# Filler products in free PSUM tiles, and turns at the port of VectorE and GpSimd, in a scheduled two-layer attention kernel

## The chip, the cores and the metric

The kernel runs on one core of a Trainium2 chip. The metric is the device time of one execution in microseconds (us). A core has five engines with an instruction list each: TensorE (PE in the profile, with its weight loads as PEld), VectorE (DVE), ScalarE (ACT), GpSimd (POOL) and SyncE (SP), which here only issues DMAs. Every list is worked off in the order in which the kernel wrote it, and engines wait for each other on semaphores.

## The reference

Four blocks follow each other on x of 2048 tokens by 512 columns (bf16): A, B, A, B, each with a layer norm ahead and a residual sum behind it. "Layer" L below is one pair of A and B. There are 32 heads of 16 columns.

```python
# A: attention inside 4 segments of 512 tokens, with a memory of the segments before
for s in range(4):
    p = softmax(qs @ ks.T / 4 + causal_mask)
    a_dot = p @ vs
    a_mem = (phi(qs) @ M) / (phi(qs) @ z + 1e-6)      # phi(t) = t + 1 if t > 0 else exp(t)
    o = g * a_mem + (1 - g) * a_dot                    # g = sigmoid(beta), by head
    M += phi(ks).T @ vs;  z += phi(ks).sum(tokens)
x = x + concat(o) @ wo
# B: linear attention over all tokens, features from softmax of +p and of -p
phi_q, phi_k = feat(q @ w_phi), feat(k @ w_phi)
kv, z = phi_k.T @ v, phi_k.sum(tokens)
x = x + ((phi_q @ kv) / (phi_q @ z + 1e-6)) @ wo
```

In B, kv and z run over all tokens, so no query of B can be finished before the last key has been added.

## The kernel before

Tokens come in 16 tiles of 128, four to a segment. For each layer the kernel projects q, k and v of a segment (`a_proj`, labels K, Q, V), works through its four tiles (`a_att`), adds the output projection to x (`out_proj`), normalizes again (`ln`) and adds B's keys of the segment to KV32 (`b_keys`). After the fourth segment the queries of B follow, four chunks of four tiles (`b_query`), mixed with the norms and projections of the next layer's A. This is called the pass to queries below; there is one for each layer.

In `a_att` a score product of TensorE (pQ,pK) fills a PSUM tile of 128x1024, ACT takes its exponential into SBUF (L603), GpSimd masks the diagonal tiles (L1035), TensorE multiplies with the values (pV), and VectorE divides (L649, L1063). In segment 0 of layer 0 the scores need a q masked by head (Q4), which VectorE makes at L969. VectorE's copies of the layer A weights into their working order are L804, the gate on the value weights L792. In `b_query` the denominators (Rz) come first. From them ACT and VectorE make weights (L1213 to L1219); the numerators (Rkv) are computed per tile, copied by ACT, multiplied at L1236, transposed by TensorE against ident or by a DMA, and projected with WB_o. All matmuls of these steps are recorded at L593. PSUM holds four tiles of 128x1024 (pool pD, in the profile D), with caps by class: at most two live tiles of class S, to which scores and numerators belong.

The order is not written by hand. Each step is recorded as an operation with a price in ns for each engine that may take it, with what it reads and writes. `Graph.forward` then plays all engines forward in time: at each moment every free engine takes the ready operation of highest priority whose tiles can be had. Priorities come from a backward pass, and are then shifted by a list of random seeds (STEPS). What comes out is an order for each engine, and the choice of engine for copies that ACT or VectorE may do (`evac`). `emit` writes the lists with a semaphore wait for each dependence. Prices and planned times are not in the program.

Two rules of `forward` matter here. One is on the port shared by VectorE and GpSimd: a VectorE operation marked `port` isn't started while GpSimd is at work, and GpSimd not while such an operation runs. When both are free, VectorE is asked first, as it stands first in ENGS. The other is on TensorE's activity: if fewer than 60% of the columns possible (KEEP) were streamed in the last 3 us (WINDOW), the next operation with columns of 64 or more repeats its first product until that is made up, at most 1024 columns a pair (MORE):

```python
lack = KEEP * WINDOW * 2.4 - streamed - o.cyc
o.again = min(MORE * 512 // o.unit, max(0, int(-(-lack // o.unit))))
```

At the start of the program `warm` (L917) sends 56 products of a constant tile of ones (onesb), 64x512 each, into a PSUM tile.

## Time and profile before

| | |
|---|---|
| median of 8 runs | 547.04 us (544.58 to 552.81) |
| the profiled execution | 547.03 us, of which the span of instructions is 545.3 us |
| mean granted TensorE clock | 0.984 |
| busy: PE, ACT, DVE, POOL | 473.9, 470.7, 440.0, 232.1 us |
| POOL waits for the exponentials of ACT (L1035) | 156.4 us |
| ACT waits for TensorE at L603 | 46.2 us in 56 waits |
| moved by DMA | 31.79 MB, 58 GB/s in the mean |

The page divides the span into 40 slices of 13.6 us; a digit is the busy share of an engine there in tenths, and in the row PEclk the share of the full TensorE clock that was granted. Time that an engine idles matters only where a later step waits for that engine.

### The profile page before, as it was taken

To read this page: it belongs to the slowest core of one execution; us is meant where nothing else is said; L and a number is where in the kernel's file an instruction comes from. 1 tells how busy PE (TensorE), PEld (TensorE's weight loads), DVE (VectorE), ACT (ScalarE), POOL (GpSimd) and SP (SyncE) were. 2 spreads that over 40 slices of the span, in tenths; PEclk is the share of its full clock that TensorE was granted. 3 is DMA by queue.
4 is the path that set the end of the run, shared out by engine and by line. 5 is a ranking of instruction groups with operands and counts; after the bars stand their busy time and mean duration, and the time that the engine had idled before them with its cause. 6 is when DMAs were issued, how large, how long until landed. Compare 5 with 4: busy or idle time off the path is not lost.

```text
span 545.3 us, 25035 instructions
## 1 busy us (share of the span) xinstructions
PE 473.9 (87%) x11338; PEld 286.2 (52%) x11338; DVE 440.0 (81%) x853; ACT 470.7 (86%) x547; POOL 232.1 (43%) x401
## 2 busy tenths in 40 slices
PE   8868788899898899997998888997989998899785
PEld 3325344555464565656753655454555555465674
DVE  6898998997986987776786989897788797878771
ACT  3959988999999999677787989999989999886884
POOL 5645767445653753100326634763463384310000
PEclk9979999999999999997899999999999999999999
DMA  7155343622211211000224445324021112100265
GB/s 213 31 183 133 71 83 73 81 49 61 42 33 32 33 32 31 4 1 5 32 63 83 64 96 74 70 42 80 31 42 25 40 23 41 26 9 3 52 119 127
DMA packets 90521, 31.79 MB, mean 58 GB/s; under 512 B 77584, under 2 KB 90416, under 8 KB 90416
## 3 DMA queue, kind: packets, MB, share of 16 engines
q1 hardware_dynamic: 90352, 30.17, 27.4%
q8 instruction: 89, 1.46, 1.2%
q14 instruction: 16, 0.13, 0.1%
q0 software_dynamic: 64, 0.02, 0.0%
HBM read 6.32 MB, written 2.10 MB: 15 GB/s over the span
## 4 chain that ended last, share of the span: by engine, by line
PE 43%; DVE 23%; ACT 21%; DMA 8%; issue 4%; SPq 1%; POOL 0%; DVEq 0%; ACTq 0%
PE D L593 41%; ACT p L603 19%; DMA p<-p 7%; DVE p L1063 2%; DVE p L612 2%; DVE p L869 2%; DVE stats L848 2%; PE D L917 2%; DVE pQ L969 1%; DVE X L1096 1%; DVE p L1236 1%; DVE pS L1141 1%; DVE pS L649 1%; DVE pK L612 1%; SPq L975 1%
## 5 line engine op out<-in xcount | busy, mean ns | idle before, releaser
L603 ACT ACTIVATE p<-D 128x1024 bf16<-128x1024 f32 (+1 forms) x420 | 400.5, 1025 | 50.0 <-PE D L593 46.2
L1035 POOL TENSOR_SCALAR_AFFINE_SELECT p<-p 128x512 bf16<-128x512 bf16 x256 | 163.8, 666 | 156.8 <-ACT p L603 156.4
L593 PE MATMUL D<-pQ,pK 64*128 64x512 bf16 x676 | 124.3, 379 | 15.8 <-ACT p L603 11.2
L593 PE MATMUL D<-pV,p 64*128 64x34 bf16 x5312 | 94.0, 177 | 5.0 <-issue 1.7
L593 PEld LDWEIGHTS D<-pV,p 64*128 64x128 bf16 x5312 | 82.8, 93 | 19.2 <-issue 5.6
L593 PEld LDWEIGHTS D<-pQ,pK 64*128 64x128 bf16 x676 | 32.7, 94 | 49.1 <-ACT p L603 27.1
L856 POOL TENSOR_SCALAR rstd<-mv 128x1 f32<-128x1 f32 x60 | 16.6, 280 | 93.5 <-DVE mv L849 92.0
L1063 DVE TENSOR_TENSOR p<-D,pS 128x256 bf16<-128x256 f32 x112 | 47.2, 422 | 2.9
L593 PE MATMUL D<-WA_o,p 64*128 64x256 bf16 x532 | 40.2, 270 | 8.4 <-DMA p<-p 5.3
L848 DVE BATCH_NORM_STATS2 stats<-X 128x6 f32<-128x512 bf16 x64 | 43.4, 685 | 4.3 <-DMA X<-in_A_x_dram 2.3
L1141 DVE TENSOR_REDUCE pS<-p 128x64 f32<-128x1024 bf16 (+1 forms) x36 | 38.7, 1087 | 6.7 <-ACT p L603 6.7
L593 PE MATMUL D<-WB_o,p 64*128 64x256 bf16 x522 | 40.4, 278 | 4.3 <-DMA p<-p 1.9
L1161 DVE TENSOR_TENSOR pT<-D,pT 128x1024 bf16<-128x1024 f32 x32 | 38.7, 1213 | 5.5 <-PE D L593 5.1
L593 PE MATMUL D<-WA_v,pX 64*128 64x512 bf16 x258 | 34.8, 392 | 6.1 <-DVE pV L612 4.1
L858 POOL TENSOR_TENSOR rstd<-rstd,mhalf 128x1 f32<-128x1 f32 x60 | 36.6, 612 | 3.4
L593 PE MATMUL D<-WB_k,pX 64*128 64x512 bf16 (+1 forms) x288 | 34.6, 353 | 3.2 <-issue 1.7
L593 PEld LDWEIGHTS D<-WA_o,p 64*128 64x128 bf16 x532 | 23.5, 94 | 22.0 <-DMA p<-p 8.5
L593 PE MATMUL D<-WB_v,pX 64*128 64x512 bf16 (+1 forms) x290 | 34.0, 354 | 0.8 <-DVE pT L649 0.4
L593 PE MATMUL D<-pX,WA_q 64*128 64x512 bf16 x228 | 29.7, 382 | 5.3 <-DVE p L1243 2.1
L1096 DVE TENSOR_TENSOR X<-X,D 128x512 bf16<-128x512 bf16 x32 | 21.8, 682 | 15.3 <-PE D L593 14.8
L649 DVE RECIPROCAL pS<-D 128x32 f32<-128x32 f32 (+1 forms) x64 | 20.7, 324 | 15.3 <-PE D L593 14.9
L593 PE MATMUL D<-pX,WB_q 64*128 64x512 bf16 x256 | 32.1, 376 | 0.1
(114 smaller groups left out, 681.7 us busy)
## 6 DMA issues: line engine op xcount, KB each, us to landing
pQ<-p SPq DMA_DIRECT2D x112, 32.0 KB, 1.8
out_dram<-X SPq DMA_DIRECT2D x16, 128.0 KB, 2.0
X<-in_A_x_dram SPq DMA_DIRECT2D x3, 512.0 KB, 4.9
pX<-in_B_wqkv_dram SPq DMA_DIRECT2D x3, 512.0 KB, 5.7
p<-p SPq DMA_TRANSPOSE x76, 2.7
pX<-p SPq DMA_TRANSPOSE x54, 2.4
X<-in_A_x_dram SPq DMA_DIRECT2D x4, 128.0 KB, 2.6
pX<-in_A_wk_dram SPq DMA_DIRECT2D x2, 256.0 KB, 3.6
```

Of the source, the lines that this page charges most:

```text
L593: ins = e.matmul(out_ap, lhsT, rhs, start=st, stop=sp, tile_position=(basep(lhsT), 0))
L603: return self.g.op({"act": (dur, lambda e: e.activation(out_ap(), in_ap(), func, scale=scale))}, reads, writes, opens, label=label)
L612: "dve": ((340 if fast else n / 0.96 + 65), lambda e: e.tensor_copy(out_ap(), in_ap()))}
L649: return e.reciprocal(o, i)
L848: v(lambda e: e.bn_stats(self.stats[:, t, :], self.X[:, t, :]), 602, [R("X", t)], [R("st", t)], label="bn")
L856: v(lambda e: e.tensor_scalar(rs, self.mv[:, t, 1:2], LN_EPS, None, op0=ALU.add), 170, [R("mv", t)], [R("rstd", t)], eng="pool", label="rstd")
L858: v(lambda e: e.tensor_tensor(rs, rs, self.mhalf[:], ALU.pow), 540, [R("rstd", t), R("mhalf")], [R("rstd", t)], eng="pool", label="rstd")
L1035: v(lambda e, pt4=pt4: e.affine_select(pt4(), pt4(), [[0, 4], [1, 128]], ALU.is_ge, 0.0, base=0, channel_multiplier=-1), 560, [PT], [PT[hh ...
L1063: v(lambda e, pvv=pvv, rden=rden, part=part, dst=dst, k=k: e.tensor_tensor(part(dst), pvv()[:, :, k, :, 0:16], rden()[:, :, k, :, None].to ...
L1096: self.v(lambda e: e.tensor_tensor(xt(), xt(), res(), ALU.add), 602, [R("X", t), ps], [R("X", t)], label="res")
L1141: fn = lambda e, sgn=sgn, ev=ev, Z=Z, nz=nz: e.tensor_reduce(Z.t[:, sgn * nz:(sgn + 1) * nz], ev().rearrange("p (h d) -> p h d", d=16), AX ...
L1161: v(lambda e, Vt=Vt, src=src, vt=vt: e.tensor_tensor(vt(Vt, 0, 16), src(), vt(Vt, 16, 17).to_broadcast([128, 2, 2, 2, 16, 8]), ALU.mult), ...
```

## The change

1. When TensorE finds nothing to do in the plan, after the first 12 us, and a PSUM tile is free, under 70% (IDLE) of the columns were streamed in the last 3 us, and no TensorE operation that could have its tiles becomes ready within 216 ns (FILL), the planner puts in a filler: two products of the tile of ones, 64x512 each, written into the free tile. The tile isn't reserved by this; the filler waits for the tile's last readers.
2. When VectorE and GpSimd are both free, the one is asked first that did not hold the port last (TURNS).
3. Some prices change: a load issued on SP from 470 ns to 520 (or 620 each, in groups), two kinds of copy on ACT and VectorE.
4. The list STEPS is another one, with 137 seeds in place of 108.

```diff
+TURNS = {"pool": ENGS, "dve": ("pe", "act", "pool", "dve", "sp")}
-WINDOW, KEEP, MORE = 3000.0, 0.6, 2
+WINDOW, KEEP, MORE, IDLE, FILL, START = 3000.0, 0.6, 2, 0.7, 216.0, 12000.0
+    def filler(self, now):
+        pool, make, deps = self.idle
+        o = Op()
+        o.id, o.deps, o.tiles, o.opens, o.hard, o.kind, o.label = 0, set(deps), [], [], (), "c", "fill"
+        t = Tile(pool, "fill")
+        t.base, t.slot = pool.base[pool.free[0]], pool.free[0]
+        o.tiles = [t]
+        o.ch = {"pe": (FILL, lambda e: make(e, t.t))}
...
-            for e in ENGS:
-                if free[e] > now + 1e-9 or not ready[e]:
+            for e in TURNS[port_last]:
+                if free[e] > now + 1e-9 or not (ready[e] or e == "pe"):
                     continue
...
+                    if e == "pe" and self.idle and now > START and len(self.idle[0].free) > 0:
+                        while seen_pe and seen_pe[0][0] < now + FILL - WINDOW:
+                            streamed -= seen_pe.pop(0)[1]
+                        if streamed < IDLE * WINDOW * 2.4 and not any(r < now + FILL and ops[i].eng is None and can_alloc(ops[i]) for r, i in soon[e]):
+                            o = self.filler(now)
+                            seen_pe.append((o.end, 512.0))
+                            streamed += 512.0
+                            free[e] = o.end
...
-                    held_port = o.end
+                    held_port, port_last = o.end, e
+                elif e == "pool" and o.kind == "c":
+                    port_last = e
...
-    def evac(self, out_ap, in_ap, n, reads, writes, opens=(), label="", fast=False):
-        ch = {"act": (n / 1.2 + 51, lambda e: e.activation(out_ap(), in_ap(), ACT.Copy)),
+    def evac(self, out_ap, in_ap, n, reads, writes, opens=(), label="", fast=False, slow=0):
+        ch = {"act": (slow or n / 1.2 + 51, lambda e: e.activation(out_ap(), in_ap(), ACT.Copy)),
...
-            dur = 780.0 if eng == "pool" else 470.0
+            dur = 780.0 if eng == "pool" else 520.0 if n == 1 else 620.0
...
+    def fill(self, e, ps):
+        for b in range(2):
+            ones = self.onesb[64 * b:64 * b + 64, :]
+            ins = e.matmul(ps[:, 512 * b:512 * b + 512], ones, ones[:, None, :].to_broadcast([64, 4, 128]), start=True, stop=True, tile_position=(64 * b, 0))
+        return ins
...
+        self.g.idle = self.pD, self.fill, list(self.R("onesb").w)
         self.g.schedule(self.pools, ROUNDS, OFF)
```

In the changed program the fillers are recorded at L953, and the line numbers behind `filler` stand some 28 to 35 lines further on (L593 becomes L621, L603 becomes L631, L969 becomes L1003).

## The prediction

> **What bounds the kernel now.** I read the page's busy times and slices first, then the waits, then windows around every dip in the clock row, then the timeline and the chain there.

> ```profile
> span 545.3 us, 25035 instructions
> PE 473.9 (87%) x11338; PEld 286.2 (52%) x11338; DVE 440.0 (81%) x853; ACT 470.7 (86%) x547; POOL 232.1 (43%) x401
> PEclk9979999999999999997899999999999999999999
> ACT p L603 <- PE D L593: 46.2, 56, 4.5
> PEld D L593 <- DMA pX<-p: 6.6, 2, 4.6
> ```

> No engine is saturated. ACT idles for 545.3 − 470.7 = 74.6 us, and most of that (46.2 us) is the exponential waiting for TensorE, once for 4.5 us. The kernel is held by hand-overs between engines, so the question is where they are worst. The clock row dips in its third digit (27 to 41 us, where the mean is 0.75) and in digits 19 and 20 (245 to 273 us). The mean clock of 0.984 means 0.016 x 545.3 = 8.7 us of clock lost, that is about 17 us at half speed. Windows cut at the edges:

> ```profile
> 31.30:35.40 4.10, 0.01 (x3) 0.03 (x1) 4.10 (x10) 1.94 (x2) 1.29 (x2) 0.81 0.27 46
> 35.40:40.80 5.40, 5.40 (x27) 2.15 (x29) 4.22 (x10) 1.94 (x2) 1.23 (x2) 0.51 1.06 370
> 245.40:252.50 7.10, 4.89 (x316) 4.58 (x316) 5.08 (x14) 6.28 (x12) 0.00 (x0) 0.99 0.02 5
> 252.50:262.70 10.20, 8.77 (x240) 7.27 (x240) 5.15 (x11) 5.36 (x10) 0.00 (x0) 0.51 0.07 16
> ```

> The columns are length, then busy time of PE, weight loads, DVE, ACT and POOL, then the granted clock. TensorE does nothing for 4.1 us and then works 5.4 us without a pause at half clock. Around 245 us, where layer 0 passes from its last keys to its queries, it is busy 4.89 of 7.10 us with tiny matmuls, and then spends 10.2 us at half clock, busy 86% of it. These are the two places that the fillers can reach. What stands in the first:

> ```profile
> 35.37 0.16 PEld L593 LDWEIGHTS D<-WA_v,pX 64*128 64x128 bf16 x4 [4.55 <-DMA pX<-p]
> 37.75 1.02 ACT L603 ACTIVATE p<-D 128x1024 bf16<-128x1024 f32 x1 [4.46 <-PE D L593]
> ```

> The value projection of segment 1 stands in TensorE's list ahead of scores of segment 0. It waits for DMA transposes, everything behind it waits too, and ACT loses 4.46 us.

> **The change part by part.**

> *Fillers.* In the built program of the changed kernel, 88 matmuls of 64x512 (44 fillers of two) are added: 26 among the scores of segment 0 in layer 0, 28 at the first pass to queries, 2 in layer 1, 28 at the second pass to queries and 4 near the end. They replace repeats: Rkv products fall from 680 to 512, ident products from 348 to 238, WB_o from 522 to 512; score products (pQ,pK) rise from 676 to 698. A filler is not in the trace. The nearest rows are WA_v products of the same shape: 16 of them took 1.89 us and 8 took 1.03, so one more costs 0.86/8 = 0.108 us; the upper end is the warm-up row (9.1 us for 56, 0.163 each, partly cold). With 0.108: fillers 88 x 0.108 = +9.5 us, score repeats 22 x 0.108 = +2.4. What is dropped:

> ```profile
> 246.64 2.01 PE L593 MATMUL D<-Rkv,p 64*128 64x64 bf16 x124 [0.25 <-DVE Rkv L1114]
> 507.37 0.87 PE L593 MATMUL D<-ident,p 64*128 64x64 bf16 x48 [0.37 <-DVE p L1236]
> ```

> That is 16 ns per Rkv and 18 ns per ident product: 168 x 0.016 = 2.7, 110 x 0.018 = 2.0, and 10 WB_o about 0.6 us. TensorE's net work is +6.6 us. It is nearly free only where it lies in idle time: PE has 71 us of that. A filler waits for the last reader of its PSUM tile (an ACT or DVE copy), as does the product behind it on the same tile; so it adds no wait, but it stands 0.2 to 1.1 us in front of that product. Queued behind are the numerators (Rkv), and for them waits ACT's copy, then the VectorE multiply at L1236. In a plan that runs late this is lost time; that cover gone, it costs the full 9.5 us.

> *First pass to queries.* What full clock is worth there, the trace itself shows, since the same stage runs a second time at clock 1.00:

> ```profile
> 245.44 0.96 PE L593 MATMUL D<-Rz,p 64*128 64x8 bf16 x64 [0.83 <-DVE Rz L1117]
> 261.39 1.06 PE L593 MATMUL D<-WB_o,p 64*128 64x256 bf16 x8
> 502.58 0.95 PE L593 MATMUL D<-Rz,p 64*128 64x8 bf16 x64
> 513.51 0.61 PE L593 MATMUL D<-WB_o,p 64*128 64x256 bf16 x8
> ```

> From the first Rz product to the end of the third half of an output projection: 262.45 − 245.44 = 17.0 us against 514.12 − 502.58 = 11.5 us. The first passage holds 104 more Rkv products (1.7 us), 48 more ident (0.9) and 64 fewer Rz (−1.0), so 5.5 − 1.6 = 3.9 us is the clock. As a bound from above: 8.77 us of PE at half clock would shrink like WB_o's 1.06 to 0.61, by 3.7 us, and 1.8 us more if the waits before it go too: 5.5. From below: 0, should it dip again. Taken −4.0. The repeats dropped there (some 100 pairs, 3.5 us) and the 14 fillers (3.0 us) cancel.

> [...] But at 252.5 us the longest gap before the fall is under 2 us: small products alone did not hold the clock. [...]

> *The start.* The diff reprices a load on SP (470 to 520 or 620 per issue), and the built order puts the segment 1 value projection behind 15 score tiles of segment 0 where it stood behind 7, and behind the 13 fillers. SP is moved too: weight loads of layer B now stand between the four transposes of segment 1, and the first transposes of weights follow earlier. The 4.46 us of ACT wait, with the 1.1 and 0.5 that follow under half clock, is 6.1 us at most. VectorE is next: the chain before 35.3 us is its masks and copies (L969, L804), and it is busy 12.28, 12.42 and 11.27 us of the three slices from 13.6 to 54.5 us, leaving 4.9 us. So the gain is between −4.9 and, if the masks come later than the scores, +2. VectorE's work there hardly changes: one gate of WA_v comes from GpSimd (+1.2), three weight copies leave for ACT (−1.4). Taken −3.0. Late next: the masks of Q4.

> *Second pass and end.* The clock was 1.00 there, so 32 fillers can gain nothing: +3.5 us of PE work against about 1.4 us of repeats gone, in a stretch where PE is busy 33.1 of 43.0 us. Bounds 0 and +2.1; taken +0.5. SP's last transposes change from four in a row to three, a store and one: within ±1, taken 0. The very last filler only follows the last projection: 0.

> *Turns at the port.* Nothing in the program enforces a turn: the planner reorders, and no semaphore is added. What overlap costs shows in one row at two times:

> ```profile
> 21.26 0.41 DVE L969 TENSOR_TENSOR pQ<-p 128x512 bf16<-128x512 bf16 x1
> 25.46 0.85 DVE L969 TENSOR_TENSOR pQ<-p 128x512 bf16<-128x512 bf16 x1
> ```

> The slower one runs beside GpSimd's mask. Over all rows (16 of L969 at 582 against 410 ns, 48 of L869 at 496 against 400, L905 and L1067) the surplus is about 10 us of VectorE, some 3 of it before 68 us where VectorE is on the path. Bounds −3 and +3, taken 0.

> *The rest of the order.* Nearly every list is permuted, since the planner's seeds change. Work per engine hardly moves (DVE +2.4, ACT −0.6 us from the copies that change sides), and both engines have 75 us or more idle. Over 41 to 218 and 300 to 491 us ACT's idle slices sum to about 22 us; a permutation may win or lose a quarter of that, ±5. Taken −0.5, as two of the copies now priced dearer leave ACT (0.74 us each, L611): an estimate from these rows, no more.

> Sum: −4.0 − 3.0 + 0.5 + 0 − 0.5 = −7.0 us on a span of 545.3: 538.3, with 1.7 around it 540.0. The profiled execution took 547.03, the median 547.04, so no shift is needed.

> **The rivals.**
> *Slower: fillers in front of due work.* All 44 sit on PSUM tiles that a numerator or score is about to use. If ACT's copies come earlier than planned or the inputs are ready, each filler is a pure delay: +9.5 us, less 4.7 us of repeats dropped, no clock won: 547 + 5 = 552. It decides only where the clock isn't won, and then from 4.7 us of filler on the path, as much as the dropped repeats give back. For it: that product carries no wait of its own in several groups. Against: ACT and DVE idle at the passes because they wait on each other (the 1.8 us before 252.98 is not PE's).
> *The clock falls all the same, or the next wait takes the gain.* Fillers come in bursts of 0.2 to 1.1 us, and 14 of them add 7,168 columns a row half over 15 us. If that is too thin, the first pass gives 0, and a start held by VectorE gives −1: 546. For it: the repeats were meant for the same and failed. Then the change doesn't do what it says.
> *The order wins more.* Both places give their bounds (−4.9, −5.5) and the permutation −5: about 531.

> **How the numbers follow.** Forecast 0.60 (own range 533 to 546, mostly faster); next wait or clock 0.17 (mostly same); fillers or a worse order on the path 0.19 (547 to 553); order wins more 0.04. Within 0.5% is 544.3 to 549.8, about what a measurement of this kernel can tell from no change. Faster: 0.55 + 0.05 + 0.04 = 0.64. Same: 0.05 + 0.11 + 0.01 = 0.17. Slower: 0.18 + 0.01 = 0.19. The range runs from the best case, 531, to the price of the slower one, 552.

> **What would show it.** Right: clock at or above 0.99 with no slice under 0.9 between 27 and 41 and between 245 and 273 us; the 4.5 us ACT wait gone; first Rz to third half projection in 12 to 13.5 us; L969 still above 500 ns. Wrong: the clock restored with the end unmoved (the wait moved on), TensorE's wait on ACT at L953 followed at once by Rkv rows with ACT idle (fillers in the way), or a gain that lies between 45 and 220 us (the order).

## The result, and the profile after

The changed kernel takes 543.47 us in the median (540.65 to 550.45) where the kernel before took 548.19 beside it: a ratio of 0.9928 (0.9906 to 0.995), some 3.9 us less. Measured again on another chip it is 0.9913 (0.9874 to 0.9952). Chips differ by up to 3.7 us in the median of the kernel before (547.10 to 550.78 us beside the experiments), so kernels are compared by their ratio to the kernel before of the same chip. Ratios leave disturbed runs out, so where a kernel's runs spread widely its ratio lies below what its median says (e9 and e16 below). The profiled execution after was one of the longer of its kernel: 548.0 us. Its page (the same rows as shown of before) and its waits (us in all, times, longest):

```profile
span 546.2 us, 24666 instructions
PE 479.0 (88%) x11156; PEld 284.4 (52%) x11156; DVE 430.0 (79%) x854; ACT 468.4 (86%) x547; POOL 234.8 (43%) x400
PEclk9978999999999999999999999899999999999899
...
ACT p L631 <- PE D L621: 49.4, 53, 4.2
PE D L621 <- issue: 10.2, 9, 3.7
```

The dip of the clock row at 245 to 273 us is gone, the one at 27 to 41 us is not, and there are new ones in digits 4, 26 and 38: half clock at 43.9 to 47.4, 351.1 to 354.6 and 515.0 to 518.4 us, where before ran at full clock. VectorE has lost 10 us of work, and the span hardly shows it. ACT waits as long as before. The pass to queries has changed in kind (window of after from the first Rz product to the end of the third half projection; then the timeline inside):

```profile
249.41:259.52 10.11, 9.41 (x352) 7.27 (x352) 6.94 (x17) 9.93 (x18) 0.00 (x0) 1.00 0.02 5
...
250.53 1.24 PE L953 MATMUL D<-onesb 64*128 64x512 bf16 x10
253.31 0.26 PE L621 MATMUL D<-Rz,p 64*128 64x8 bf16 x8 [0.21 <-issue]
254.54 1.25 PE L953 MATMUL D<-onesb 64*128 64x512 bf16 x10
258.92 0.60 PE L621 MATMUL D<-WB_o,p 64*128 64x256 bf16 x8
```

TensorE is busy 9.41 of 10.11 us at full clock: 17.0 us have become 10.1. So 6.9 us were won here, and this execution's span shows none of it. A table by stage, from the starts and ends in the traces (us; "again" is a second profile of the changed kernel, the last column an experiment told of below):

| stage | before | after | again | old order, shifted |
|---|---|---|---|---|
| start to the end of the second sum into X | 58.8 | 58.9 | 54.3 | 59.1 |
| to the first Rz product, layer 0 | 186.6 | 190.5 | 189.7 | 186.8 |
| to the third half projection | 17.0 | 10.1 | 10.0 | 11.5 |
| to the first Rz product, layer 1 | 240.1 | 243.8 | 244.2 | 236.4 |
| to the end | 42.7 | 42.9 | 44.3 | 39.3 |

The changed order gives back 3 to 4 us in each of the two long stages, and its start differs by 4.6 us between two executions of one program.

### The profile page after: what moved, and what is told of

Its sections match the earlier page's. It is cut to its first block, busy times and chain, and to the rows that moved or that the text cites. A ratio compares the mean times of both kernels' runs of the same rounds, so it can differ in the third digit from the quotient of the medians.

```text
span 546.2 us, 24666 instructions
## 1 busy us (share of the span) xinstructions
PE 479.0 (88%) x11156; PEld 284.4 (52%) x11156; DVE 430.0 (79%) x854; ACT 468.4 (86%) x547; POOL 234.8 (43%) x400
## 4 chain that ended last, share of the span: by engine, by line
PE 49%; ACT 23%; DVE 11%; DMA 10%; issue 3%; POOL 2%; SPq 1%; ACTq 0%
PE D L621 47%; ACT p L631 20%; DMA p<-p 7%; DMA pX<-p 3%; PE D L945 2%; DVE p L1097 2%; POOL p L1069 1%; DVE p L640 1%; SPq L1009 1%; DVE X L1130 1%; DVE pS L677 1%; DVE stats L876 1%; DVE pS L1175 1%; DVE pT L1195 1%; DVE p L897 1%
## 5 line engine op out<-in xcount | busy, mean ns | idle before, releaser
L631 ACT ACTIVATE p<-D 128x1024 bf16<-128x1024 f32 (+1 forms) x420 | 399.5, 1028 | 53.4 <-PE D L621 49.4
L621 PE MATMUL D<-pQ,pK 64*128 64x512 bf16 x698 | 129.1, 385 | 11.9 <-ACT p L631 10.1
L621 PE MATMUL D<-pV,p 64*128 64x34 bf16 (+1 forms) x5312 | 94.4, 177 | 9.1 <-issue 3.8
L621 PEld LDWEIGHTS D<-pV,p 64*128 64x128 bf16 x5312 | 82.8, 93 | 23.1 <-issue 10.0
L884 POOL TENSOR_SCALAR rstd<-mv 128x1 f32<-128x1 f32 x60 | 18.1, 304 | 101.9 <-DVE mv L877 101.9
L621 PEld LDWEIGHTS D<-pQ,pK 64*128 64x128 bf16 x698 | 34.1, 94 | 43.9 <-ACT p L631 24.0
L621 PE MATMUL D<-WA_o,p 64*128 64x256 bf16 x534 | 40.2, 271 | 10.9 <-DMA p<-p 8.0
L621 PE MATMUL D<-WB_o,p 64*128 64x256 bf16 x512 | 39.2, 274 | 6.6 <-DMA p<-p 4.9
L621 PE MATMUL D<-WA_v,pX 64*128 64x512 bf16 x256 | 33.9, 385 | 6.1 <-issue 3.7
L621 PE MATMUL D<-WB_k,pX 64*128 64x512 bf16 (+1 forms) x288 | 34.2, 353 | 4.5 <-DMA pX<-p 3.1
L621 PEld LDWEIGHTS D<-WA_o,p 64*128 64x128 bf16 x534 | 22.6, 94 | 27.1 <-DMA p<-p 12.4
L621 PE MATMUL D<-WB_v,pX 64*128 64x512 bf16 (+1 forms) x288 | 33.5, 353 | 0.9 <-ACT p L631 0.4
L621 PE MATMUL D<-pX,WB_q 64*128 64x512 bf16 x256 | 32.5, 376 | 0.1
L621 PE MATMUL D<-pX,WA_q 64*128 64x512 bf16 x224 | 29.3, 377 | 3.1 <-issue 1.6
```

The source lines that it names most:

```text
L621: ins = e.matmul(out_ap, lhsT, rhs, start=st, stop=sp, tile_position=(basep(lhsT), 0))
L631: return self.g.op({"act": (dur, lambda e: e.activation(out_ap(), in_ap(), func, scale=scale))}, reads, writes, opens, label=label)
L884: v(lambda e: e.tensor_scalar(rs, self.mv[:, t, 1:2], LN_EPS, None, op0=ALU.add), 170, [R("mv", t)], [R("rstd", t)], eng="pool", label="rstd")
```

## What the timeline of before had shown all along

The two rows of before that matter most were not read rightly in the prediction. Here they are, with their neighbours (timeline, PE alone; "issue" means that the engine waited for nothing that the profile shows):

```profile
249.25 0.29 PE L593 MATMUL D<-Rkv,p 64*128 64x64 bf16 x8 [0.60 <-issue]
...
250.83 0.35 PE L593 MATMUL D<-ident,p 64*128 64x64 bf16 x12
252.99 1.14 PE L593 MATMUL D<-ident,p 64*128 64x64 bf16 x36 [1.81 <-issue]
...
255.44 0.65 PE L593 MATMUL D<-Rz,p 64*128 64x8 bf16 x36
256.99 0.54 PE L593 MATMUL D<-Rz,p 64*128 64x8 bf16 x28 [0.91 <-issue]
```

Three times TensorE stops in the middle of a group (12 and 36 products of one transpose, 36 and 28 of one denominator). Nothing in the program waits there. Number TensorE's weight loads, products and semaphore waits in the order of their start: the three stand at numbers that leave 193 over a multiple of 256. So do, within two, 107 of the 129 stops of 0.5 us or more inside a group in all 20 traces of this case (score groups left out); 15 of the other 22 are one stop of the changed kernel and its variants at 22 us. The DMA part of the page of before, and of its window from 250 to 252 us, point to the cause:

```profile
q8 instruction: 89, 1.46, 1.2%
```
```profile
DMA packets 1, 0.02 MB, mean 8 GB/s; under 512 B 0, under 2 KB 0, under 8 KB 0
...
q8 instruction: 1, 0.02, 3.9%
```

1.46 MB in 89 packets are 16.4 KB each, and TensorE's 22,866 instructions in this trace (11,338 loads, as many products, 190 that wait or drain) by 256 are 89.3: by these counts TensorE's own list arrives by DMA, in blocks of 256 instructions. The only packet of that window is one of them. In the DMA records it starts at 250.37 us, 1.1 us after the block before it was entered (249.25), lands at 251.60, and TensorE goes on at 252.98. At the nine pauses of before (they are counted below) the packet starts 0.6 to 1.7 us after the block ahead was entered, and TensorE goes on 1.2 to 1.6 us after it has landed, so that the new block begins 3.1 to 4.2 us after the previous one. The trace doesn't say what a packet holds; that it is the next block is read from these times. The same block can pause in one execution and not in another: at one place after waited 1.40 us for a packet that started 2.8 us late (186.43 us), and in its second profile, where the packet started at once, not at all.

Below, a "block pause" is a gap of at least 0.5 us between the starts of two TensorE instructions at such a number, where the 256 before took under 4 us. Before has 9 of them, 10.3 us in all; after 5, 6.7 us; the second profile of after 3, 4.4 us. They come where short products use up the list fast: at the nine of before the 256 instructions ahead took 1.7 to 3.3 us without the pause, and 124 Rkv products passed in 2.01 us are, with their loads, 248 instructions. Fillers of 512 columns use it up more slowly: 10 of their products, with the loads 20 instructions, took 1.24 us in after. But every product added or dropped also moves all later block starts to other places; the last two experiments separate that from everything else.

## Experiments

There are four theories. *Clock*: the fillers hold the clock. *Order*: the gain is the new order's. *In the way*: fillers stand in front of due work. *Blocks* (later): what counts is where the block starts fall. The expectations number them: theory 1 is always the clock; 2 is the order (in e4 no change, in e7 the seeds); 3 is "in the way" in e1 to e3 and "blocks" in e17 and e18. "Clock lost" is (1 − granted clock) x span, a mean over all runs of a kernel; before has 11 us, after 7. Pauses are of the one profiled execution; that of e9 was one of its long ones (555.5 us).

### Fillers dropped or doubled

```diff
+at = [k for k, o in enumerate(self.g.order) if o.label == "fill"]
+drop = set(at)                   # e1: all 44
+drop = set(at[:13] + at[27:])    # e2: only the 14 of the first pass stay
+drop = set(at[:13])              # e9, e16: without the 13 of the start
+drop = set(at[28:])              # e10: without the 16 of the second pass and the end
+self.g.order = [o for k, o in enumerate(self.g.order) if k not in drop]
```
```diff
 def fill(self, e, ps):            # e3
-        for b in range(2):
+        for b in (0, 1, 0, 1):
```

e1: 

> The order of the changed kernel, with the 44 fillers left out of the lists. If the fillers give the gain by holding TensorE's clock (theory 1), the first pass to queries (first Rz product to the end of the third half of a WB_o projection, 10.1 us in the changed kernel's profile, 17.0 before) goes back to 14 to 17 us with half clock in it, and the time is 548 to 552 us, no better than before. If the new order gives it (theory 2), the time stays within 1.5 us of the changed kernel, 542 to 545. If fillers stand in the way of due work (theory 3), it is faster than the changed kernel: 537 to 541.

e2: 

> The changed kernel with only the 14 fillers of the first pass to queries; the 13 at the start and the 17 later ones are left out. Theory 1 (only the first pass had a clock to win): as fast as the changed kernel within 1.5 us, 542 to 545, with the first pass at 10 to 11 us. Theory 2: the same number, but then the run without any filler gives it too. Theory 3: 1 to 3 us faster than the changed kernel. If the start's fillers matter, 2 us slower with more half clock before 50 us.

e3: 

> Every filler of the changed kernel has four products in place of two: 88 more products of 0.108 us, +9.5 us of TensorE work at the same places. Theory 3 (fillers lie in front of due work): 5 to 9.5 us slower than the changed kernel, 548 to 553. Theories 1 and 2 (they lie in idle time): within 2.5 us of it, 541 to 546, with the last stretch (first Rz product of the second pass to the end) longer by no more than 2 us.

e9: 

> The changed kernel without its 13 fillers at the start; the other 31 stay. The runs so far fit a span of about 536 us plus 0.9 times the clock lost (1 minus mean clock, times the span: 6.9 us in the changed kernel, 13.2 with the first pass's fillers alone, 17.5 with none). If the start's fillers are what makes the difference between the first pass's fillers alone (552.8 us) and all (543.5), this is 549 to 553 us with 12 us or more of clock lost. If it is the second pass's fillers, 542 to 546. If both share it, 546 to 549.

e10: 

> The changed kernel without the 16 fillers of the second pass to queries and after it; the start's 13, the first pass's 14 and one in layer 1 stay. The prediction held these to be a cost of 0.5 us: by it, 542 to 544, slightly faster. If they hold a clock that the new order would lose there (half clock at 509 to 513 us in the profile of the kernel with the first pass's fillers alone), 546 to 550, with 3 us or more of clock lost on top.

e13: 

> The changed kernel as it is, beside the next three on one chip. Theory 1 (the fillers hold the clock and are all of the gain, the order is neutral): 0.990 to 0.996 of before. If the earlier 0.993 was drawn from a lucky chip, 0.997 or above.

e16: 

> The changed kernel without the 13 fillers of the start. If these carry most of what is won: 4 to 8 us above the changed kernel of the same chip, with 3 us or more of clock lost in addition. If the first pass carries it, as the forecast had it: within 2 us of the changed kernel.

| kernel | median | before beside it | ratio | clock lost | block pauses |
|---|---|---|---|---|---|
| e1, no fillers | 554.77 | 547.27 | 1.0111 (1.0056 to 1.0167) | 17.5 | 7, 6.5 us |
| e2, first pass only | 552.81 | 547.27 | 1.0105 (1.0069 to 1.0142) | 13.2 | 8, 8.0 |
| e3, doubled | 545.04 | 547.27 | 0.9943 (0.9907 to 0.998) | 4.6 | 5, 6.0 |
| e9, none at the start | 552.24 | 547.10 | 1.0000 (0.9956 to 1.0043) | 10.0 | 10, 9.6 |
| e10, none at the second pass | 541.26 | 547.10 | 0.9891 (0.9841 to 0.9942) | 7.8 | 5, 5.6 |
| e13, after again | 542.89 | 547.43 | 0.9913 (0.9874 to 0.9952) | 7.1 | 3, 4.4 |
| e16, none at the start | 549.64 | 547.43 | 1.0013 (0.9969 to 1.0057) | 9.4 | 8, 8.0 |

Doubling adds 9.5 us of TensorE work by the prediction's price and costs at most 2 us net, with 2.3 us less clock lost, so the fillers lie mostly in idle time: "in the way" falls. Without fillers the new order is slower than the old one and loses 10 us more clock than with them. The expectations of e1 and e2 were missed: e1 is slower than 548 to 552 although its first pass takes 11.9 us and not 14 to 17, and e2, with the first pass's fillers alone, is 8 us off the 542 to 545 of the clock theory, which its 8 pauses may explain. e9 and e16 came out as if the start's fillers carried the gain, but e16 loses only 2.3 us more clock than e13. What the fillers do at the first pass shows in the windows of e1, then of e2:

```profile
245.80:253.20 7.40, 5.53 (x230) 3.80 (x230) 4.24 (x12) 6.80 (x13) 0.00 (x0) 1.00 0.01 2
253.20:260.10 6.90, 5.65 (x119) 4.82 (x121) 5.30 (x12) 5.71 (x8) 0.00 (x0) 0.51 0.02 5
```
```profile
246.40:253.20 6.80, 6.71 (x222) 4.14 (x224) 4.00 (x10) 6.19 (x10) 0.00 (x0) 1.00 0.01 2
253.20:260.10 6.90, 6.31 (x238) 5.21 (x236) 6.41 (x16) 6.67 (x13) 0.00 (x0) 1.00 0.02 5
```

Without them TensorE is busy 5.53 of 7.40 us and the next 6.9 us run at half clock (the third figure from the end is the granted clock); with them 6.71 of 6.80 us and the clock stays. So they do hold it. The second pass says the same: without its fillers (e1, e2, e10, e15) the clock fell 4.4 to 5.1 us after the pass's first Rz product in all four profiles, with them in none of ten that early, though in after and e13 it fell some 12 us behind it. From the first Rz product to the third half projection, e1 takes 11.9 us, e2 10.0, before 17.0: of the 6.9 us won, 5.1 come without any filler, since the short repeats are gone and with them the three block pauses (3.85 us), and the half clock lasts 6.9 us instead of 10.2. The fillers' clock is worth the other 1.9.

The puzzle was e16: slower than e13 by 5.5 us by the ratios (6.7 by the medians), although its start was not much later (56.2 us to the second sum into X, 54.3 in e13). In the profiles it loses 3.3 us up to the first pass and 1.4 more up to the second, where the two lists are the same product for product.

### The old order with long fillers

```diff
+if o.eng == "pe" and o.again and o.unit == 64:     # repeats of 64 columns
+    n, o.again = -(-o.again * o.unit // 512), 0
+    ... n pairs of 64x512 of the ones go ahead of the operation, into its own tile
```

> The kernel before in its own order; wherever it repeats a product of 64 columns (139 pairs in all), fillers of 512 columns with the same sum of columns stand in their place (21 fillers, the last of each group rounded up). Theory 1, in the form that long products count for the clock and short ones do not: the half clock at 252 to 262 us is gone, the first pass falls from 17.0 to 11 to 13 us, and the time is 542 to 545. Theory 2: no change, 546 to 549. If equal columns do equally little for the clock, the half clock stays and the time is that of before.

547.19 us, 0.9978 (0.9945 to 1.0011). Clock lost fell from 11.5 to 6.9 us, as in the changed kernel, in the profile none of it at the first pass, and the pass took 11.6 us, as theory 1 had it; yet the time hardly moved. 9 block pauses, 10.4 us: as many as before, at other places. A clock that is held was not enough.

### The start

```diff
+pv = [o for o in pe if o.label == "PV"][:2]        # behind the next two score tiles
+later = [o for o in pe if o.label == "S" and o.seq > pv[1].seq][:2]
+v = [o for o in pe if o.label == "V"][4:6]         # v[0] next to v[1]
...
+order[k:k] = pv
+order.insert(order.index(v[1]), v[0])
```

e5: 

> The changed kernel with two moves in TensorE's list at the start: the first two PV groups, which wait 3.2 us for GpSimd's masks at 24.4 us, go behind the next two score tiles, and the first half of segment 1's value projection, which waits 3.7 us for DMA transposes at 42.4 us, goes next to its second half, behind two further score tiles. If the start was lost to these two waits (theory 1: an order that is neutral elsewhere, plus clock), the half clock at 26.9 to 33.7 and 43.9 to 47.4 us is gone, residual sum number 16 ends 3 to 5 us earlier (234.1 us in the changed kernel's profile), and the time is 538 to 541.5. If the next wait at the start is VectorE's (masks of Q4), the half clock goes but the time stays within 1.5 us of the changed kernel, 542 to 545.

e14: 

> The changed kernel with the first two products of weights and values behind the next two score tiles, and the value projection of segment 1 in the middle moved back. If the wait that moved at the start is what the forecast missed: 0.984 to 0.989 of before, and 3 to 5 us below the changed kernel of the same chip. If the 4 us later first pass is made up behind it anyway: the same as the changed kernel within 1.5 us.

e15, e14 without the 16 fillers of the second pass: 

> The start moved as above, and the 16 fillers of the second pass and behind it left out. If these fillers stand in front of due work: 1 to 2 us below the kernel with the moved start alone. If they lie in idle time: the same within 1.5 us. If they hold a clock that would fall there: 2 to 4 us above.

e11, e5 with three loads of SP behind its fourth transpose: 

> The kernel with the start moved (541.6 us), and in SP's list the three loads that stand between the four transposes of segment 1 go behind the fourth. If the value projection's remaining wait for those transposes (1.4 us at 39 us, then 3.8 us of it at half clock) is the next price, 1 to 4 us faster: 537 to 541. If the loads are needed as soon (weights of layer B, which VectorE already waited 1.2 to 1.6 us for), within 1 us or slower.

e12, e5 with the start's 13 fillers doubled: 

> The kernel with the start moved, and its 13 fillers at the start with four products instead of two. If the half clock left at 39 to 46 us is set by what was streamed just before, it goes, and the time is 537 to 541; if it comes from the wait at 39 us alone, it stays and 1.4 us of products are added: 541 to 544.

The profiled execution of after held TensorE at 27.59 us for masks that GpSimd made late; its second profile did not (after, then again):

```profile
27.59 0.90 PE L621 MATMUL D<-pV,p 64*128 64x34 bf16 x32 [3.21 <-POOL p L1069]
```
```profile
24.78 0.80 PE L621 MATMUL D<-pV,p 64*128 64x34 bf16 x32 [0.95 <-POOL p L1069]
```

So one profile misled here. Moving the waiting products gave 0.9837 (0.9792 to 0.9883) in e5 and 0.987 (0.9814 to 0.9927) in e14, against 0.9913 for the changed kernel on the chip of e14: some 3 us better by the medians (539.58 against 542.89), with intervals that overlap. e15 gave 0.9877 (0.9816 to 0.9938), so the second pass's fillers neither help nor harm the time by more than these intervals. e11 (0.9913, 0.9875 to 0.9951) and e12 (0.991, 0.9874 to 0.9946) are no better than after, so the gain of the moves themselves isn't sure.

### Seeds and turns

```diff
-STEPS = (
-    ...
+STEPS = ()
-TURNS = {"pool": ENGS, "dve": ("pe", "act", "pool", "dve", "sp")}
+TURNS = {"pool": ENGS, "dve": ENGS}    # e8 alone
```

e6, before without seeds: 

> The kernel before with an empty list of seeds: the planner's own order. If the seeds carry much of the time, 10 to 30 us slower than before, 557 to 577; if they fit the planner's prices more than the chip, within 8 us, 547 to 555. Clock lost (1 minus mean clock, times the span) like before's, 9 to 14 us.

e7, after without seeds: 

> The changed kernel with an empty list of seeds; it has 56 fillers. If fillers hold the clock in any order (theory 1), it loses 4 to 7 us of clock less than the kernel before without seeds and is 3 to 7 us faster than that one. If the gain is one of the seeds found (theory 2), both are equal within 3 us or it is slower.

e8, e7 without turns: 

> As the run before it, but VectorE is always asked first at the port (as in the kernel before); 41 fillers. If turns spare VectorE waiting at the port, its busy time is 6 to 12 us longer here than with turns (430.0 us with, 440.0 without in the two kernels' profiles). If that time is off the path, the time differs by no more than 3 us either way; if it is on the path, this is 5 to 10 us slower.

565.32 us (1.027), 565.71 (1.030) and 560.06 (1.0184, 1.0132 to 1.0236), beside 550.78 of before. e7 loses 4.0 us less clock than e6, as theory 1 had it, but is no faster: its profile has 8 block pauses of 9.9 us where e6 has 5 of 5.5. With turns VectorE works 435.3 us, without 442.6, and yet the kernel without them is faster. What turns are worth isn't settled by this: the two lists differ, and so do their block starts (8 pauses of 8.2 us in e8). Seeds are worth some 15 us in the kernel before and 20 in the changed one.

### The block starts moved

26 of the 56 warm-up products are written as two of 256 columns each. The same columns are streamed; the list ahead of all else has 26 more products, as many as the 13 dropped fillers had. In e18 it is 36, on e4.

```diff
+self.n_warm = getattr(self, "n_warm", 0) + 1
+w = 2 if self.n_warm <= 26 else 4
+for c in range(0, 4, w):
-    ins = e.matmul(ps.t[:, 512 * b:512 * b + 512], ones(b), ones(b)[:, None, :].to_broadcast([64, 4, 128]),
+    ins = e.matmul(ps.t[:, 512 * b + 128 * c:512 * b + 128 * (c + w)], ones(b), ones(b)[:, None, :].to_broadcast([64, w, 128]),
```

e17: 

> The changed kernel without the 13 fillers of the start, but with 26 of the 56 warm-up products written as two of 256 columns each, so that TensorE's list holds 26 more products ahead of the first score and every later instruction stands at the same number in the list as in the changed kernel. In all traces so far a pause of 0.5 to 2 us stands at instruction numbers that are 193 or 194 over a multiple of 256, where the 256 before took under 2.7 us; the run without the start's fillers has 11 such blocks, the changed kernel 4. Theory 3 (the start's fillers count only by where they put these blocks): 0.988 to 0.995 of before, with pauses at the places of the changed kernel. Theory 1 (they hold the clock): 1.000 as without them.

e18: 

> The old order with 21 long fillers in place of its short repeats (measured 0.998), and 36 of the 56 warm-up products written as two of 256 columns. By the trace of the unshifted kernel this moves its block starts from places where the 256 instructions before took under 2.7 us (8 of them, about 8.7 us of pauses) to others (1 of them, about 0.7 us). Theory 3: 0.983 to 0.993 of before, so the old order does as well as the new. If the pauses lie off the path: 0.998 as before the shift. If the new order is needed for the gain: not below 0.995.

e17: 544.91 us beside 549.08, 0.9922 (0.9885 to 0.996), against 1.0013 unshifted and 0.9913 with the fillers. So nothing can be measured of the start's fillers beyond the places to which they push the block starts: theory 3. e16, then e17, timeline of PE:

```profile
173.57 0.50 PE L621 MATMUL D<-pV,p 64*128 64x34 bf16 x27 [1.08 <-issue]
...
226.34 0.51 PE L621 MATMUL D<-pV,p 64*128 64x34 bf16 x27
227.92 0.38 PE L621 MATMUL D<-pV,p 64*128 64x34 bf16 x17 [1.07 <-issue]
...
380.83 0.51 PE L621 MATMUL D<-pV,p 64*128 64x34 bf16 x27
382.54 0.32 PE L621 MATMUL D<-pV,p 64*128 64x34 bf16 x11 [1.20 <-issue]
```
```profile
170.84 0.76 PE L621 MATMUL D<-pV,p 64*128 64x34 bf16 x48
...
223.89 0.97 PE L621 MATMUL D<-pV,p 64*128 64x34 bf16 x64
```

The first two of these groups run through uncut in e17; 4 pauses of 5.2 us are left of 8 of 8.0.

e18: 539.19 us, 0.9806 (0.9756 to 0.9855), the lowest ratio of all kernels run, in the old order (the interval of e5, 0.9792 to 0.9883, overlaps it). Page and waits of e4, then of e18:

```profile
span 544.1 us, 24535 instructions
PEclk9989999999999999999999999999999999999999
...
ACT p L603 <- PE D L593: 47.0, 61, 3.5
PE D L593 <- issue: 12.9, 13, 2.2
```
```profile
span 533.2 us, 24607 instructions
PEclk9989999999999999999999999999999999999999
...
ACT p L603 <- PE D L593: 37.7, 48, 3.6
PE D L593 <- issue: 3.3, 4, 1.7
```

Here order, fillers and clock row are the same (one piece of half clock less, some 1.7 us), and 36 more products in the list move the span by 10.9 us. The start itself is no faster (59.1 us to the second sum into X, 57.3 in e4), so the split warm-up isn't what wins. TensorE's unexplained waits fall by 9.6 us, ACT's waits for TensorE by 9.3: the pauses lie on the path nearly one for one. 1 block pause of 0.6 us is left of 9. By the ratios of all runs the move is worth 1.7%, some 9 us.

## Why the prediction was half right

The direction was right, the size was not: −7.0 us were forecast, some −3.9 measured.

- **The direction and the first pass** came out as forecast, the latter larger (−6.9 for −4.0), but partly by luck. "5.5 − 1.6 = 3.9 us is the clock" measured 1.9 (e1 against e2): the first passage holds three block pauses, 3.85 us, and the second has two of its own, 1.22 and 0.50 us between starts, seen in these lines of before:

```profile
508.14 0.47 PE L593 MATMUL D<-Rkv,p 64*128 64x64 bf16 x19
509.64 0.37 PE L593 MATMUL D<-Rkv,p 64*128 64x64 bf16 x13 [1.03 <-issue]
...
513.38 0.21 PE L593 MATMUL D<-Rz,p 64*128 64x8 bf16 x5 [0.34 <-issue]
```

The difference of 2.1 us was taken for clock; without it 1.8 us are left, close to the 1.9. (The count of products has a slip too: both passages hold 192 Rz products, and what the second has more are 8 of WB_q, 1.02 us, so that the −1.0 stands by chance.) That "the 1.8 us before 252.98 is not PE's" was wrong: it was PE's own list that was missing. That the dropped repeats and the fillers "cancel" failed with it: 5.1 us came in e1 with the repeats gone and no filler in their place.
- **Small products and the clock.** e1 bears out what the trace of before showed, that small products alone did not hold the clock: it fell at 253.2 us with no gap above 1.4 us between starts in the 8 us before. A thin flow was enough here, TensorE busy 5.53 of the 7.40 us ahead of the fall. In the gap at 31 us of before the clock fell 2.55 us after TensorE had stopped: the window from 31.30 to 33.85 us has it at 1.00, the one from 33.85 to 40.68 at 0.50.
- **The start** (−3.0): +0.1 in one profile, −4.5 in the other, with or without fillers (54.6 and 56.2 us in e9 and e16). The 4.5 us wait of ACT did not go (4.2 after), and the profile's mean clock stayed at 0.984 where 0.99 was expected (over all runs, clock lost fell from 11 to 7 us). The size lies between the two profiles, and its cause was the order, not the fillers.
- **The rest of the order** (−0.5) is the term that failed: +3.1 to +3.9 us up to the first pass and +3.7 to +4.1 up to the second, +7.2 to +7.6 together. The bound of ±5 was too narrow, and it rested on ACT's idle time alone. What stands in these two stages (us; half clock counted as half its length):

| two long stages | before | after | again |
|---|---|---|---|
| time | 426.7 | 434.3 | 433.9 |
| block pauses | 3.5 | 6.7 | 4.4 |
| lost to half clock | 0 | 1.7 | 5.1 |
| what is left | 423.2 | 425.9 | 424.4 |

If each counts one for one (an estimate), pauses and half clock at new places make 4.9 to 6.0 us of the loss, and the prediction had a term for neither: the pauses sat in a row of waits that was not read (`issue`), and the clock was taken to stay full where it was full before. The other 1.2 to 2.7 us are the order's own; their cause stays open.
- **Second pass** (+0.5) and **turns** (0): nothing measurable in the second pass (e10, e15). No run isolates the turns; VectorE works 9 to 10 us less in after and e13, and no stage shows it. A port that VectorE and GpSimd share is the planner's premise. What the trace of before shows is longer rows: of the 16 of L969 the 9 that lie more than half beside GpSimd's work took 0.71 us in the mean, the other 7 took 0.42.
- **Rivals.** "Fillers in front of due work" is refuted by e3. Nearest to what happened is "the next wait takes the gain", though the waits were ones that none of the rivals had.

How much of the change's 3.9 us is clock and how much luck with block starts can't be split cleanly, since each filler does both. An estimate: a least-squares line through the 14 kernels in the new order with seeds (e1 to e3, e5, e9 to e17 and after; the span as a mean of the runs, the pauses of one profile each) gives 0.9 us of span for each us of clock lost and 1.2, give or take 0.5, for each us of block pause, with 1.9 us of scatter. With 4 us less clock lost and 3.6 to 5.9 less pause it would make −8 to −11 us, 4 to 7 more than was measured; that much would be lost to the order, more than the 1.2 to 2.7 of the table, so the two estimates agree only roughly. What is shown is that the old order, with long fillers and its block starts moved, does better than the changed kernel, so the new order isn't needed for the gain. The new order with its block starts moved to places as good was not run.

## What to carry to other kernels

Before an order is judged, look for "issue" waits of 0.5 us or more in the middle of a group, and number the engine's instructions: if they stand 256 apart, put other instructions ahead (in e18 36 split warm-up products moved the span by 10.9 us) and compare several offsets, or two schedules are compared by the luck of where their blocks fall. Try few long products in place of many short ones to hold the clock: in e4 21 fillers with the columns of 139 short pairs cut the clock lost from 11.5 to 6.9 us, and short products use up the list (124 of them 248 instructions in 2.01 us). And take two profiles before a stage is explained: the changed kernel's start had half clock at 26.9 to 33.7 and 43.9 to 47.4 us in one and at 39.2 to 42.6 us in the other, and 5 block pauses of 6.7 us against 3 of 4.4.
